# Fourteen weight pieces of an attention and feed-forward kernel: their decoding spread from attention cycle 40 to cycle 58

## The chip, the core and the metric

The kernel runs on one core of a Trainium2 chip. The core has five engines that run side by side, each through its own instruction list in order: TensorE (PE, matrix products; PEld is its loading of weights), VectorE (DVE), ScalarE (ACT), GpSimd (POOL), and SyncE (SP), which here issues the transfers. The metric is the device time of one execution in microseconds (us), the median of several runs.

## What is computed

The input is 64 heads (8 batches of 8) of 576 positions by 64 channels. Attention keeps, in each row of scores, only those within tau of the row's maximum. The result, seen as 4608 tokens by 512 channels, goes through two layers with a slope per hidden unit for negative values.

```python
scores = matmul(q, k.T) / sqrt(64)
thresh = max(scores, -1) - tau
scores = where(scores >= thresh, scores, -1e9)
attn   = softmax(scores)                # 8 x 8 heads, 576 x 576
x      = (attn @ v) as 4608 x 512
h      = x @ w_in                       # 512 x 2048
g      = maximum(h, 0) + alpha * minimum(h, 0)
out    = g @ w_out                      # 2048 x 512
```

The weights w_in and w_out arrive as 64-bit floats.

## The kernel before

**Pairs, units, cycles.** Heads are taken two at a time: 32 pairs, 9 units each (a unit is 128 query rows by 576 keys; one unit of a pair holds what is left over of both heads). The loop at the end of the program runs over cycles i from -3 to 296, and cycle i does the middle step of unit i % 9 of pair i // 9. In it DVE masks the scores of unit i (`mask`, line 438), PE makes the scores of unit i + 2 (`scores`, line 403) and turns the masked rows of unit i by transposes (`turn`, line 447), ACT and DVE copy the turned rows to SBUF, DVE takes the row maximum (`rowmax`, line 418) and ACT the exponential (`expo`, line 426). The scores lie in two PSUM buffers, so that the scores of unit i + 2 wait for the mask of unit i. Products with the values (`avmul`, line 550) come at fixed cycles. Pairs 0 to 3 ("whole") keep the turned rows in one 32-bit copy. From pair 4 on they are split into a high part that ACT copies (line 499) and a rest that DVE subtracts (line 503), one such subtraction per turned tile.

**Fixed order.** The lists of PE, DVE, ACT and POOL are written by hand: what stands earlier in the program text stands earlier in the list. Steps can be set for a cycle by `at_cycle(c, step)`. Transfers on SP are ordered by the compiler.

**Weights.** A weight piece is 128 columns of w_in or 128 rows of w_out, 128x512 words of 64 bits. The class `Split64` turns one into two 32-bit tiles, a high part and a rest. `decode_at(c, ...)` spreads one piece over seven cycles: at c ACT makes two tiles of it (`size`, lines 125 and 126), at c+1 to c+4 DVE has one instruction a cycle (`clamp` line 129, `shift` line 132, `sign` line 137, `power` line 142), at c+4 ACT also rounds (`round`, line 146), at c+5 POOL multiplies and subtracts (`rest`, lines 150 and 151), at c+6 POOL adds (`join`, line 154). These four DVE instructions are called decoding instructions below; i0 to i6 are the pieces of w_in, o0 to o6 those of w_out. A piece of w_in is loaded up to 12 cycles ahead (`LD`), one of w_out 3 cycles ahead. Seven pieces of each weight are decoded during the attention; the other nine of each follow after it and aren't touched by the change.

**Where the words lie.** The raw words of o0 to o5 lie in the place of a later weight tile; those of o6 in a ring of two buffers ("raw") that the loads of q, k and v use as well. The temporary words (`wt`) of a piece lie in a ring of four in the pool `spool`. At cycle 41 (`SPC`) that pool is closed, and its memory goes to the pool `mp1` of the feed-forward part. A piece that begins later takes its temporary words from the ring `g` of `mp1`, which has 11 buffers (`GB`) and otherwise holds the activations between the two layers.

**Feed-forward beside the attention.** As soon as all heads of a batch are done, groups of 256 tokens are fed in: `Mlp.step_l1` (first layer, 7 blocks of 128 hidden units) and `Mlp.step_l2` (second layer), as far as a planner finds room on PE in a cycle (`room`, a budget of 2.6 us). Group 0 is fetched at cycle 49 and its first block starts at cycle 52. A first layer is admitted only while fewer than `GB` activations are in use (`live`). All that is left of the feed-forward follows after the last unit.

The first fourteen pieces before: a piece of w_in every 3 cycles from -3 on, a piece of w_out every 3 cycles from 16 on.

```python
for n_, (w, fc, io) in enumerate(pieces):
    c = DEC0 + DEC * n_ if n_ < F1 else DECO0 + DECO * (n_ - F1)
    load = max(-3, c - LD) if io == "i" else c - 3
    decode_at(c, wp1, w, fc, io, load if n_ else None)
```

Of the kernel before, what the change touches and what calls it, by code (L numbers as in the profile page):

```python
# [25 lines left out]
F1 = 7  # L26
# [9 lines left out]
GB = 11  # L36
# [14 lines left out]
ACTO, SPLO, PUTO = 1, 2, 1  # L51
TH1, TH2, TH3 = 0.75, -0.45, 0.1
XO = 1
L2O = 3
P1 = 2
LD = 12
# [1 line left out]
WHOLE = 4  # L58
EVP = (0, 0, 0, 1)
EVD = lambda i: EVP[i % len(EVP)]  # L60
DEC0, DEC = -3, 3
DECO0, DECO = 16, 3
RDY = 13
CYCLE = 2.6

# [1 line left out]
def f(ap):  # L67
    return ap.bitcast(F32)
# [3 lines left out]
def tile_masked_attention_moe(  # L72
# [31 lines left out]
    class Split64:  # L104
# [12 lines left out]
        def size(self):  # L117
            words = self.raw.bitcast(I32).rearrange("p (n two) -> p n two", two=2)
            self.low, self.high = words[:, :, 0], words[:, :, 1]
            tag, bufs = self.temp_tag  # L120
            pool = self.temp_pool
            if pool is mem:
                pool, tag, bufs = (mem.mp1, "g", GB) if mem.mp1 else (spool, "wt", 4)
            self.t = pool.tile([P, DM], I32, tag=tag, name=f"wt{self.name}", bufs=bufs)
            nc.scalar.activation(f(self.t), f(self.high), AF.Abs)
            nc.scalar.activation(f(self.low), self.low.bitcast(U32), AF.Copy, scale=2.0**-52)

        def clamp(self):
            self.eng[0].tensor_scalar(f(self.t), f(self.t), WORD_LO, WORD_HI, op0=ALU.max, op1=ALU.min)
# [22 lines left out]

        def join(self, lo):
            nc.gpsimd.tensor_tensor(lo, f(self.t), f(self.low), op=ALU.add)

    def src_i(fc):
        return w_in[:, fc * P : (fc + 1) * P].rearrange("(cc p) f -> p cc f", p=P), NCC, f"i{fc}"
# [80 lines left out]
    wp1 = p1.enter_context(tc.tile_pool(name="wp1", bufs=1, side="right"))  # L238
    sp = ExitStack()
    spool = sp.enter_context(tc.tile_pool(name="spool", bufs=1, side="right"))  # L240
    mem = SimpleNamespace(mp1=None)
    at, ps = ExitStack(), ExitStack()
    ap1 = at.enter_context(tc.tile_pool(name="ap1", bufs=1))
    ps_m = ps.enter_context(tc.tile_pool(name="ps_m", bufs=4, space=PSUM))
# [410 lines left out]
    class Mlp:  # L655


        def __init__(self):
            self.l1, self.l2 = deque(), deque()
            self.acc = None  # L660
            self.live = 0
            self.gap = 0
            self.room = 0.0

# [7 lines left out]
        def step_l1(self, i):  # L672
            gi, st, fi = self.l1.popleft()
# [4 lines left out]
                self.gap = i + XO + 2  # L678
                return
            name = f"a{gi}_{fi}"  # L680
            self.live += 1
            ph = layer1(ps_m, fcs1[fi], n, st["x"], name)

            alone = i >= total
# [20 lines left out]
        def step_l2(self, i):  # L705
            _, gi, st, o, fj, ti = self.l2.popleft()
            t0, n = groups1[gi]
            m = min(P, n - o)
            if fj == 0 and ti == 0:
                self.acc = ps_m.tile([P, 512], F32, tag="pm", name=f"acca{gi}_{o}")  # L710
            acc = self.acc
            layer2(acc, fcs1[fj], st["g"][fj], o, m, fj == 0, fj == F1 - 1, (ti,))
            if ti < 2:
                return
            if o + P >= n:
                self.live -= 1
            if fj == F1 - 1:

                def put():
                    po = mem.mp1.tile([P, DM], F32, tag="po", name=f"po{gi}_{o}", bufs=1)  # L720
                    nc.scalar.activation(po[:m], acc[:m], AF.Copy)
                    nc.sync.dma_start(part[gi][o : o + m, :], po[:m])

                first_at_cycle(i + PUTO, put)

        def cycle(self, i, used, slot):

            self.room = min(self.room, TH3) + CYCLE - used
            l1 = False
            if self.l1 and i >= self.gap and self.live < GB:  # L730
                if self.l1[0][2] is None:
                    self.step_l1(i)
                elif slot and self.room > TH1 and ("i", fcs1[self.l1[0][2]]) in ready:
                    l1 = True
                    self.room -= 1.31
# [37 lines left out]
        at_cycle(c + 6, lambda: (w.join((wi if io == "i" else wo)[fc][:, 1]), ready.add((io, fc))))  # L773

    for n_, (w, fc, io) in enumerate(pieces):
        c = DEC0 + DEC * n_ if n_ < F1 else DECO0 + DECO * (n_ - F1)
        load = max(-3, c - LD) if io == "i" else c - 3
        decode_at(c, wp1, w, fc, io, load if n_ else None)

# [259 lines left out]
```

## Time and profile before

| | |
|---|---|
| median of three runs | 1379.86 us (1378.5 to 1380.6) |
| the profiled execution | 1380.41 us, its span 1378.6 us |
| busy in the span | PE 97%, DVE 72%, ACT 61%, POOL 59% |
| chain of work that ended last | PE 85%, DVE 6%, ACT 4% |

The chain of work that ended last is followed back from the last instruction to whatever released each step. Most of the span is PE's. The page's row of DVE shows 6 tenths in the first of 40 slices, 8 or 9 in the next 23, and less behind them; that of PE shows 5 to 8 tenths in the first five slices, and 9 from there on. So the stretch in which PE isn't full is the first 170 us or so, in which the weights are decoded. The time and the span differ by 1.8 us, which lies around the program.

### The profile page before, as it was taken

What the parts mean: (1) busy time and instruction counts of PE and PEld (TensorE: products, weight loads), DVE (VectorE), ACT (ScalarE), POOL (GpSimd) and SP (SyncE); (2) the same over time, 40 slices, a digit from 0 to 9 for tenths busy, and PEclk for the clock granted to TensorE, in tenths of its full rate; (3) what the DMA queues carried; (4) which work ended last, traced back from release to release, by engine and by line L of the source; (5) the groups of instructions that cost most, each with busy time, mean ns of one, the idle gap of its engine ahead of it and who ended that gap; (6) DMA issues with size and microseconds to landing.
All of it is one profiled execution on the core that took longest, in us unless ns stands there. A gap on an engine that the chain in (4) does not pass through costs nothing.

```text
span 1378.6 us, 23959 instructions
## 1 busy us (share of the span) xinstructions
PE 1332.7 (97%) x8116; PEld 1180.2 (86%) x8116; DVE 994.5 (72%) x1970; ACT 842.5 (61%) x1915; POOL 814.9 (59%) x891
## 2 busy tenths in 40 slices
PE   5888899999999999999999999999999999999998
PEld 4556789999999999999999998898888888888887
DVE  6999888888888888889888883883655644333332
ACT  6878888888888888888888873542323321211210
POOL 3776566666666575766666654884757554443431
PEclk9999999999999999999999999999999999999999
DMA  8644643644643644445445413345455452343222
GB/s 252 173 138 112 164 110 109 175 124 112 172 135 114 167 126 128 141 133 142 132 129 150 120 55 110 117 144 169 156 181 187 134 184 92 102 152 113 92 77 77
DMA packets 115178, 186.05 MB, mean 135 GB/s; under 512 B 18320, under 2 KB 49328, under 8 KB 115056
## 3 DMA queue, kind: packets, MB, share of 16 engines
q1 hardware_dynamic: 115056, 184.52, 45.2%
q8 instruction: 65, 1.06, 0.3%
q14 instruction: 57, 0.47, 0.1%
HBM read 104.41 MB, written 37.90 MB: 103 GB/s over the span
## 4 chain that ended last, share of the span: by engine, by line
PE 85%; DVE 6%; ACT 4%; issue 1%; DMA 1%; POOL 1%; SPq 0%; POOLq 0%; DVEq 0%; ACTq 0%
PE accj L232 19%; PE phj L196 18%; PE av L550 11%; PE s L403 11%; PE acca L232 9%; PE pha L196 9%; PE t L447 7%; DVE p L438 2%; DVE nmx L418 1%; PE tk L463 1%; DMA wri<-in_moe_w_in_dram 1%; ACT xb L563 1%; ACT xa L561 1%; ACT xh L182 1%; ACT p L426 0%
## 5 line engine op out<-in xcount | busy, mean ns | idle before, releaser
L418 DVE TENSOR_REDUCE nmx<-s 128x1 f32<-128x576 f32 x288 | 217.2, 754 | 73.2 <-PE s L403 70.1
L223 ACT ACTIVATE gj<-ptj 128x512 fp32r<-128x512 f32 (+1 forms) x109 | 62.9, 577 | 338.1 <-DVE ptj L215 338.1
L226 POOL TENSOR_TENSOR gj<-ptj,gj 128x512 fp32r<-128x512 f32 (+1 forms) x109 | 129.2, 1186 | 237.2 <-ACT gj L223 236.5
L232 PE MATMUL accj<-wo,gj 128*128 128x512 f32 x1140 | 262.4, 390 | 0.6 <-POOL gj L226 0.6
L232 PEld LDWEIGHTS accj<-wo,gj 128*128 128x128 f32 x1140 | 213.9, 188 | 45.1 <-POOL gj L226 1.0
L196 PE MATMUL phj<-xhj,wi 128*128 128x512 f32 (+1 forms) x816 | 232.8, 367 | 0.0
L438 DVE SCALAR_TENSOR_TENSOR p<-s,thr,p 128x576 f32<-128x576 f32 x256 | 206.8, 808 | 1.6 <-ACT thr L431 1.2
L426 ACT ACTIVATE p<-s,nmx 128x576 f32<-128x576 f32 x256 | 190.1, 742 | 10.2 <-DVE nmx L418 9.9
L232 PE MATMUL acca<-wo,ga 128*128 128x512 f32 x588 | 186.1, 423 | 1.6 <-POOL ga L226 0.8
L403 PE MATMUL s<-kh,qst 128*128 128x288 f32 x640 | 142.5, 313 | 38.3 <-DVE p L438 22.1
L196 PEld LDWEIGHTS phj<-xhj,wi 128*128 128x128 f32 x816 | 147.6, 188 | 25.2
L214 DVE TENSOR_SCALAR ptj<-phj,alpha_sb 128x512 f32<-128x512 f32 (+1 forms) x109 | 74.2, 681 | 124.4 <-PE phj L196 120.4
L196 PE MATMUL pha<-xh,wi 128*128 128x256 f32 x784 | 156.9, 284 | 0.2 <-ACT pra L209 0.2
L447 PE MATMUL t<-ident,p 128*128 128x128 f32 x1024 | 154.8, 274 | 0.0
L403 PEld LDWEIGHTS s<-kh,qst 128*128 128x128 f32 x640 | 101.6, 193 | 61.2 <-issue 31.2
L196 PE MATMUL phj<-xlj,wi 128*128 128x512 f32 (+1 forms) x408 | 150.0, 368 | 1.1 <-POOL xlj L810 0.9
L962 DVE TENSOR_TENSOR obj<-accj,pinj 128x512 f32<-128x512 f32 x72 | 49.8, 692 | 138.5 <-PE accj L232 127.7
L403 PE MATMUL s<-kl,qst 128*128 128x288 f32 x640 | 133.7, 299 | 0.0
L196 PEld LDWEIGHTS pha<-xh,wi 128*128 128x128 f32 x784 | 128.1, 190 | 4.4 <-ACT pra L209 1.5
L447 PEld LDWEIGHTS t<-ident,p 128*128 128x128 f32 x1024 | 126.6, 141 | 0.1
L232 PEld LDWEIGHTS acca<-wo,ga 128*128 128x128 f32 x588 | 102.1, 192 | 13.7 <-POOL ga L226 1.2
L219 POOL TENSOR_TENSOR pta<-pta,pra 128x256 f32<-128x256 f32 x94 | 69.4, 739 | 73.9 <-ACT pra L209 71.3
(123 smaller groups left out, 2865.5 us busy)
## 6 DMA issues: line engine op xcount, KB each, us to landing
pinj<-part SPq DMA_DIRECT2D x72, 256.0 KB
kr<-in_k_dram SPq DMA_DIRECT2D x31, 320.0 KB
rb<-rvd SPq DMA_DIRECT2D x64, 144.0 KB
xs<-xa SPq DMA_DIRECT2D x32, 288.0 KB
part<-obj SPq DMA_DIRECT2D x36, 256.0 KB
out_dram<-obj SPq DMA_DIRECT2D x36, 256.0 KB
vr<-in_v_dram SPq DMA_DIRECT2D x28, 320.0 KB
qr<-in_q_dram SPq DMA_DIRECT2D x31, 288.0 KB
```

What stands on the lines that cost most here:

```text
L196: nc.tensor.matmul(ph[:, :n], w[:, c, :], xx[:, c, :n], start=(c == 0 and ti == 0), stop=(c == NCC - 1 and ti == 2),)
L214: nc.vector.tensor_scalar(t[:, :n], ph[:, :n], 0.0, alpha_sb[:, fc : fc + 1], op0=ALU.min, op1=ALU.mult)
L219: nc.gpsimd.tensor_tensor(t[:, :n], t[:, :n], r[:, :n], op=ALU.add)
L223: nc.scalar.activation(g[:, 0, :n], t[:, :n], AF.Copy)
L226: nc.gpsimd.tensor_tensor(g[:, 1, :n], t[:, :n], f(g[:, 0, :n]), op=ALU.subtract)
L232: nc.tensor.matmul(acc[:m, :], gg[:, g, o : o + m], w, start=(first and ti == 0), stop=(last and ti == 2))
L403: nc.tensor.matmul(ps[:, h, :288], w, kk[:, a + h * 288 : a + (h + 1) * 288], start=(ki == 0 and i == 0), stop=(ki == 1 and i == n - 1),)
L418: nc.vector.tensor_reduce(self.nmx[:, j : j + 1], self.S[u][0][:, :, :288], axis=AX.XY, op=ALU.max, negate=True)
L426: nc.scalar.activation(pj, ps[:, :, :288], AF.Exp, bias=nmx[:, j : j + 1], scale=1.0)
L438: nc.vector.scalar_tensor_tensor(pj, ps[:, :, :288], thr[:, j : j + 1], pj, op0=ALU.is_ge, op1=ALU.mult, accum_out=self.sm[:, c : c + 1])
L447: nc.tensor.transpose(tb[:, c, :], pt[:, j, j * D + c * P : j * D + (c + 1) * P], ident)
L550: nc.tensor.matmul(pa[:m, :n], w, x, start=(part == 0 and c == 0), stop=(part == z.parts[-1] and c == NKC))
```

## The change

The four constants that gave each piece its cycle are replaced by a table, with one entry for each of the fourteen pieces. The pieces of w_in now begin every 4 cycles from 1 on (the first stays at -3), o0 to o2 begin at 25, 29 and 34, and o3 to o6 at 41, 44, 48 and 52. The last four therefore take their temporary words from the ring `g`. So that activations and words together don't exceed 11 buffers, the counter `live` is replaced by a list with an entry for each tile taken from the ring, in order. An entry turns true when its tile isn't needed any more, and a first layer is admitted only if all but the last 10 entries are true.

```diff
+ROOM = GB - 1
-DEC0, DEC = -3, 3
-DECO0, DECO = 16, 3
+DECC = (-3, 1, 5, 9, 13, 17, 21, 25, 29, 34, 41, 44, 48, 52)
...
             if pool is mem:
                 pool, tag, bufs = (mem.mp1, "g", GB) if mem.mp1 else (spool, "wt", 4)
+                self.place = None
+                if mem.mp1:
+                    self.place = [False]
+                    mem.ring.append(self.place)
...
             nc.gpsimd.tensor_tensor(lo, f(self.t), f(self.low), op=ALU.add)
+            if self.place:
+                self.place[0] = True
...
-            self.live += 1
+            st["place", fi] = [False]
+            mem.ring.append(st["place", fi])
...
             if o + P >= n:
-                self.live -= 1
+                st["place", fj][0] = True
...
-            if self.l1 and i >= self.gap and self.live < GB:
+            if self.l1 and i >= self.gap and all(p[0] for p in mem.ring[:-ROOM]):
...
-        c = DEC0 + DEC * n_ if n_ < F1 else DECO0 + DECO * (n_ - F1)
+        c = DECC[n_]
```

PE's list is the same, row for row. DVE, ACT and POOL keep their instructions, at other places. The decoding instructions of DVE in the nine cycles of each pair, counted from the two tables (each piece has one at c+1, c+2, c+3 and c+4):

| pair (cycles) | 0 (0-8) | 1 (9-17) | 2 (18-26) | 3 (27-35) | 4 (36-44) | 5 (45-53) | 6 (54-62) |
|---|---|---|---|---|---|---|---|
| before | 12 | 13 | 14 | 12 | 3 | 0 | 0 |
| after | 9 | 9 | 9 | 8 | 6 | 10 | 3 |

DVE's list before at cycles 16 to 20, the end of pair 1 and the start of pair 2 (`wti` and `wto` are temporary words of w_in and w_out, `wri` and `wro` raw words, `p` the exponentials, `nmx` the row maxima, `rv` a pair's sums):

```order
L142 TENSOR_SCALAR wri_264<-wti_622 128x512
L129 TENSOR_SCALAR wti_707<-wti_707 128x512
L438 SCALAR_TENSOR_TENSOR p_3_693,sm_437<-s_8_685,thr_7_691,p_3_693 128x576
L418 TENSOR_REDUCE nmx_0_755<-s_0_716 128x1
L132 TENSOR_SCALAR wti_707<-wti_707 128x512
L129 TENSOR_SCALAR wto_743<-wto_743 128x512
...
L137 SCALAR_TENSOR_TENSOR wti_707<-wri_350,wti_707 128x512
L132 TENSOR_SCALAR wto_743<-wto_743 128x512
L438 SCALAR_TENSOR_TENSOR p_0_758,sm_715<-s_1_750,thr_0_756,p_0_758 128x576
L418 TENSOR_REDUCE nmx_2_820<-s_2_788 128x1
L142 TENSOR_SCALAR wri_350<-wti_707 128x512
L137 SCALAR_TENSOR_TENSOR wto_743<-wro_651,wto_743 128x512
```

The same engine after, at cycles 18 to 20 (the lines of the changed file are 6 to 8 higher: 135, 138, 143 and 148 are the four decoding instructions, 446 the mask, 426 the row maximum):

```order
L135 TENSOR_SCALAR wti_755<-wti_755 128x512
L446 SCALAR_TENSOR_TENSOR p_0_732,sm_697<-s_1_724,thr_0_730,p_0_732 128x576
L426 TENSOR_REDUCE nmx_2_796<-s_2_764 128x1
L138 TENSOR_SCALAR wti_755<-wti_755 128x512
L426 TENSOR_REDUCE nmx_2_796<-s_3_791 128x1
L446 SCALAR_TENSOR_TENSOR p_1_799,sm_697<-s_2_764,thr_2_797,p_1_799 128x576
L515 COPY eo_136<-t_1_802 128x4x128
L143 SCALAR_TENSOR_TENSOR wti_755<-wri_399,wti_755 128x512
```

Before, i6 and o0 overlapped, with two decoding instructions to a cycle; after, one stands in each cycle.

DVE's list before in cycles 45 to 48, at the start of pair 5:

```order
L418 TENSOR_REDUCE nmx_2_1670<-s_2_1647 128x1
L438 SCALAR_TENSOR_TENSOR p_0_1619,sm_1591<-s_1_1623,thr_0_1617,p_0_1619 128x576
L503 TENSOR_TENSOR e_117<-t_0_1655,e_116 128x4x128
L438 SCALAR_TENSOR_TENSOR p_1_1673,sm_1591<-s_2_1647,thr_2_1671,p_1_1673 128x576
L418 TENSOR_REDUCE nmx_2_1670<-s_3_1677 128x1
L503 TENSOR_TENSOR tt_121<-tk_0_1688,tt_120 128x128
L503 TENSOR_TENSOR eo_115<-t_1_1683,eo_114 128x4x128
L418 TENSOR_REDUCE nmx_4_1745<-s_4_1708 128x1
```

And after:

```order
L426 TENSOR_REDUCE nmx_2_1633<-s_2_1604 128x1
L446 SCALAR_TENSOR_TENSOR p_0_1572,sm_1543<-s_1_1576,thr_0_1570,p_0_1572 128x576
L511 TENSOR_TENSOR e_117<-t_0_1612,e_116 128x4x128
L138 TENSOR_SCALAR wto_1598<-wto_1598 128x512
L446 SCALAR_TENSOR_TENSOR p_1_1636,sm_1543<-s_2_1604,thr_2_1634,p_1_1636 128x576
L426 TENSOR_REDUCE nmx_2_1633<-s_3_1640 128x1
L143 SCALAR_TENSOR_TENSOR wto_1598<-wro_1497,wto_1598 128x512
L511 TENSOR_TENSOR tt_121<-tk_0_1651,tt_120 128x128
L511 TENSOR_TENSOR eo_115<-t_1_1646,eo_114 128x4x128
L426 TENSOR_REDUCE nmx_4_1713<-s_4_1674 128x1
```

Two decoding instructions of o4 now stand between the masks, maxima and subtractions. On ACT, in cycle 52, before the high copies (line 507, before 499) of the turned rows, the change puts the rounding of o5 and the two size instructions of o6:

```order
L344 ACTIVATE kh_1890<-kr_1820 128x640
L152 ACTIVATE wo_1895<-wto_1751 128x512
L129 ACTIVATE wto_1897<-wro_1782 128x512
L130 ACTIVATE wro_1782<-wro_1782 128x512
L507 ACTIVATE eo_114<-t_7_1880 128x4x128
```

Before, the key's copy (line 336, after 344) was followed by that high copy at once.

## Rows read from the trace of the kernel before

**Rows 1.** Busy time of each engine in seven stretches, from the first mask of a pair to the first mask of the next: pairs 0 to 6. Columns: stretch, its length, then busy us and instructions of each engine, granted PE clock, DMA share, GB/s.

```profile
14.70:37.00 22.30, 17.56 (x91) 14.06 (x92) 21.33 (x41) 19.27 (x44) 12.56 (x10) 0.92 0.81 249
37.00:63.70 26.70, 24.55 (x134) 15.99 (x133) 24.83 (x48) 22.96 (x53) 18.56 (x16) 1.00 0.61 173
63.70:91.70 28.00, 24.30 (x123) 15.66 (x122) 27.11 (x46) 20.68 (x48) 19.62 (x18) 0.94 0.48 137
91.70:118.00 26.30, 22.42 (x123) 14.83 (x122) 25.12 (x48) 22.53 (x51) 19.88 (x17) 1.00 0.45 128
118.00:141.80 23.80, 20.09 (x124) 15.19 (x122) 21.76 (x49) 19.33 (x45) 13.97 (x13) 1.00 0.41 114
141.80:166.60 24.80, 19.91 (x143) 18.91 (x142) 21.89 (x48) 21.20 (x51) 12.83 (x14) 0.93 0.64 168
166.60:191.00 24.40, 23.32 (x183) 22.60 (x183) 22.61 (x52) 21.19 (x54) 18.05 (x25) 1.00 0.44 120
```

**Rows 2.** DVE's decoding instructions in the stretch of pairs 1 to 3 (37 to 118 us), grouped by line and tile: count, busy us in all, mean ns of one, idle before.

```profile
L129 DVE TENSOR_SCALAR wto<-wto 128x512 f32<-128x512 f32 x7 | 7.2, 1035 | 0.0
L132 DVE TENSOR_SCALAR wto<-wto 128x512 int32<-128x512 int32 x6 | 7.1, 1176 | 0.0
L137 DVE SCALAR_TENSOR_TENSOR wti<-wri,wti 128x512 int32<-128x512 int32 x4 | 5.3, 1334 | 0.0
L137 DVE SCALAR_TENSOR_TENSOR wto<-wro,wto 128x512 int32<-128x512 int32 x6 | 4.2, 697 | 0.0
L142 DVE TENSOR_SCALAR wro<-wto 128x512 int32<-128x512 int32 x6 | 4.1, 692 | 0.0
...
L132 DVE TENSOR_SCALAR wti<-wti 128x512 int32<-128x512 int32 x4 | 2.3, 564 | 0.0
L142 DVE TENSOR_SCALAR wri<-wti 128x512 int32<-128x512 int32 x4 | 2.0, 495 | 0.0
...
L129 DVE TENSOR_SCALAR wti<-wti 128x512 f32<-128x512 f32 x3 | 1.3, 420 | 0.0
```

**Rows 3.** What a piece of w_out costs ACT and POOL in the same stretch, grouped in the same way.

```profile
L126 ACT ACTIVATE wro<-wro 128x512 f32<-128x512 uint32 x7 | 4.7, 672 | 0.0
L125 ACT ACTIVATE wto<-wro 128x512 f32<-128x512 f32 x7 | 4.7, 669 | 0.0
L146 ACT ACTIVATE wo<-wto 128x512 fp32r<-128x512 f32 x6 | 3.7, 622 | 1.3 <-POOL wo L154 1.3
```

```profile
L154 POOL TENSOR_TENSOR wo<-wto,wro 128x512 fp32r<-128x512 f32 x5 | 7.4, 1482 | 0.2
...
L151 POOL TENSOR_TENSOR wto<-wto,wo 128x512 f32<-128x512 f32 x5 | 6.3, 1270 | 1.4 <-ACT wo L146 1.4
...
L150 POOL TENSOR_TENSOR wro<-wro 128x512 f32<-128x512 f32 x5 | 5.7, 1134 | 2.2 <-issue 1.1 <-DVE wro L142 1.0
```

**Rows 4.** Instructions in order of time around 115 us and one at 125.68 us: start, duration, engine, line, tiles.

```profile
114.09 1.56 POOL L340 TENSOR_TENSOR kl<-kr,kh 128x640 fp32r<-128x640 f32 x1 [1.71 <-PE t L447]
...
115.07 0.87 DVE L142 TENSOR_SCALAR wro<-wto 128x512 int32<-128x512 int32 x1
...
115.60 1.49 POOL L154 TENSOR_TENSOR wo<-wto,wro 128x512 fp32r<-128x512 f32 x1
...
115.86 1.52 DVE L129 TENSOR_SCALAR wto<-wto 128x512 f32<-128x512 f32 x1
...
125.68 0.41 DVE L142 TENSOR_SCALAR wro<-wto 128x512 int32<-128x512 int32 x1
```

**Rows 5.** The chain of waits in the stretch of pairs 0 to 3 (14.7 to 118 us): shares of the stretch by engine, tile and line.

```profile
by line: PE s L403 15.4%; PE av L550 13.9%; DVE p L438 13.2%; DVE nmx L418 10.5%; PE t L447 7.1%; DVE wti L137 4.9%; issue 4.3%; DVE wto L129 4.1%; DVE wto L132 3.9%; ACT p L426 2.2%; DVE rv L568 2.2%; DVE wro L142 2.1%; DVE wti L132 1.9%; 
```

**Rows 6.** The same chain in order of time in pair 1, where it runs through PE without a break: start, length, what, instructions.

```profile
44.02 1.01 PE av L550 x4
...
45.23 1.06 PE s L403 x8
...
46.73 1.77 PE av L550 x6
48.50 0.73 PE s L403 x4
49.22 0.43 PE t L447 x4
...
49.77 1.23 PE av L550 x4
...
54.60 1.44 PE av L550 x6
```

**Rows 7.** DVE's waits in the stretch of pairs 4 to 6 (118 to 191 us): who waited for whom, us in all, times, longest.

```profile
DVE nmx L418 <- PE s L403: 3.9, 6, 1.2
DVE eo L503 <- ACT eo L499: 1.6, 5, 0.5
```

**Rows 8.** The query of pair 5, loaded through the ring that o6's raw words share: its issue on SP, and the ACT instruction that reads it, in order of time.

```profile
115.68 0.33 SPq L313 DMA_DIRECT2D qr<-in_q_dram  x1
...
119.48 0.69 ACT L353 ACTIVATE qst<-qr 128x576 fp32r<-128x576 f32 x1
```

**Rows 9.** POOL's subtraction for the first group of the feed-forward, and the first matrix product that reads it.

```profile
158.92 2.40 POOL L184 TENSOR_TENSOR xl<-xr,xh 128x1024 fp32r<-128x1024 f32 x1 [1.21 <-ACT xh L182]
```

```profile
162.80 0.28 PE L196 MATMUL pha<-xl,wi 128*128 128x256 f32 x1
```

**Rows 10.** Busy time as in rows 1, in two stretches of 3.4 us and the ones right behind them.

```profile
66.70:70.10 3.40, 1.13 (x7) 0.70 (x6) 3.40 (x6) 0.37 (x1) 1.69 (x1) 1.00 0.83 251
70.10:73.60 3.50, 3.50 (x13) 2.02 (x12) 3.50 (x8) 3.49 (x8) 3.03 (x3) 0.51 0.73 194
141.80:145.20 3.40, 1.38 (x10) 0.99 (x8) 3.37 (x9) 2.59 (x6) 1.29 (x2) 1.00 0.88 197
145.20:148.70 3.50, 2.83 (x13) 2.85 (x14) 2.83 (x7) 2.08 (x6) 1.41 (x1) 0.51 0.89 273
```

More of the change, by code (lines that the diff above doesn't have):

```diff
@@ L126, in size @@
             nc.scalar.activation(f(self.low), self.low.bitcast(U32), AF.Copy, scale=2.0**-52)
+        place = None
         def clamp(self):
@@ L240, in tile_masked_attention_moe @@
     spool = sp.enter_context(tc.tile_pool(name="spool", bufs=1, side="right"))
-    mem = SimpleNamespace(mp1=None)
+    mem = SimpleNamespace(mp1=None, ring=[])
     at, ps = ExitStack(), ExitStack()
@@ L660, in __init__ @@
             self.acc = None
-            self.live = 0
             self.gap = 0
```

## The prediction

> **What bounds the kernel now.** The chain of waits of the whole run is PE's, but the change touches only the first 60 or so cycles, so I read that part in stretches of one pair each [rows 1]. The reader is to see that DVE, not PE, is full there. In pairs 0 to 3 it is busy in 21.33 of 22.3 us, 24.83 of 26.7, 27.11 of 28.0 and 25.12 of 26.3. PE comes to a like share only in pair 6, with 23.32 of 24.4 us (before, its busy time counts products that wait in its pipeline). PE's list is unchanged, so whatever is won or lost up to cycle 60 shifts all that follows by as much.
>
> What DVE spends on decoding stands in [rows 2]: eight groups, 33.5 us for 40 instructions, so 0.84 us each. That is about twice what one takes when POOL is idle, 0.41 us [rows 4]. The other views that I read are the chain within pairs 0 to 3 [rows 5], that chain in order of time [rows 6], and the waits of DVE in pairs 4 to 6 [rows 7].
>
> **Pairs 0 to 3: work removed.** They lose 3, 4, 5 and 4 decoding instructions, 16 in all (the table in the section on the change). At 0.84 us that is 13.4 us of DVE time. Does it come off the path? For the full price speak pairs 2 and 3, which differ by two decoding instructions and by 28.0 - 26.3 = 1.7 us, 0.85 us each [rows 1]. Both are whole pairs with the same steps in the same cycles. For less speaks the chain [rows 5], which holds the decoding lines at 4.9 + 4.1 + 3.9 + 2.1 + 1.9 = 16.9% of 103.3 us, or 17.5 us. That is 17.5 us for 51 instructions, and 16 of them would be worth 5.5 us. The two ends are 13.4 and 5.5 us.
>
> There is a floor under it. Where the chain runs through PE alone, a cycle takes 0.73 us for scores and 0.43 for transposes, 0.33 more for the leftover unit of a pair (1.06 against 0.73), and a pair has two products of 1.77 + 1.23 us and two of 1.44 + 1.01 [rows 6]. That makes 9 x 1.16 + 0.33 + 6.0 + 4.9 = 21.7 us, and with the small transposes about 22 us for a whole pair. At the full price pairs 1 to 3 would fall to 23.3, 23.8 and 22.9 us. DVE would then need about 21.5 to 23 us of these, so two engines are nearly full and hand over to each other twice a cycle. I take 0.7 us off each of the three for that: **-13.4 + 2.1 = -11.3 us**, nearer to the full price, because the difference of two like pairs is a closer row than a share of a chain.
>
> **Pairs 4 to 6: work added.** The same 16 instructions come back as 3, 10 and 3. DVE has more of its own to do in these pairs (21.76, 21.89 and 22.61 us without or nearly without decoding), since the turned rows are split there. Its idle time is 2.04, 2.91 and 1.79 us, 6.7 in all. Pairs 1 to 3 keep 1.87, 0.89 and 1.18 us idle under full load, 1.3 on the mean, so I count only what is above that as cover: 0.7 + 1.6 + 0.5 = 2.8 us. The price of an instruction depends on POOL, so it is not lower here: pairs 1 to 3 have POOL busy in 58.1 of 81.0 us, 72%. Pair 5 has 12.83 us, gets two and a half pieces of 1.48 + 1.27 + 1.13 = 3.9 us [rows 3], and would have some 22.6 us in 32 or so, 71%. So **+13.4 - 2.8 = +10.6 us**. The lower end is 13.4 - 6.7 = 6.7 us, all idle time used. The upper end is 13.4 plus what ACT adds (second rival).
>
> ACT gets four pieces of 0.67 + 0.67 + 0.62 = 1.96 us, 7.8 us [rows 3], and has 4.5 + 3.6 + 3.2 = 11.3 us idle in pairs 4 to 6 [rows 1]. I cost that at nothing as long as the high copies are not late. If they are, DVE's subtractions wait.
>
> **Steps with one answer.** The list that replaces the counter admits the same layers in the same cycles, for PE's list is the same; four words and seven activations are just 11 buffers, so no tile waits for one: nothing. The raw words of o6 take one of two buffers from cycle 49 to 58, so the query of pair 7 can be loaded only when the key of pair 7 has been read. The same happened before with pair 5: its query was issued at 115.68 us, right behind POOL's reading of the key (114.09 + 1.56), and ACT read it at 119.48 without idling for it [rows 4, 8]. I take nothing, and up to 1 us if SP is held by a transfer of keys in front of it. POOL's subtraction for the first layer ended at 161.32 and PE read it at 162.80 [rows 9]; o4's rest and join come ahead of it, 3.9 us, but the cycles in front of it grow by about as much. Nothing, and up to 1.5 us.
>
> **Sum.** -11.3 + 10.6 = -0.7 us. The profiled execution took 1380.41 us, so 1379.7 in its terms. It lies 0.55 us above the median, which gives **1379.2 us** against 1379.86.
>
> **A rule beside it.** In [rows 4] a decoding instruction that began at 115.86 us ended at 117.38, 0.29 us after POOL's addition (115.60 + 1.49 = 117.09), and the one before it ended 0.29 us after POOL's earlier one (115.94 against 115.65). The Trainium skill (SBUF — State Buffer, section Who interferes with whom) says of this that DVE's two-port instructions and POOL's instructions take one shared pair of ports as an exclusive lock, so that the later one fully blocks. By that rule a decoding instruction is dear or cheap by what POOL has in hand at its start, and one to a cycle instead of two could meet POOL less often. That is the first rival.
>
> **Rivals.** *Faster: fewer meetings with POOL.* An instruction that meets none takes 0.41 us [rows 4], the dearest groups take 1.0 to 1.3 [rows 2]. With two decoding instructions in a cycle the second often starts behind the first under the same POOL work (0.87 and 1.52 us in a row [rows 4]). If one to a cycle brings the mean of all 54 from 0.84 to 0.75 us, that is 4.9 us more: 1379.2 - 4.9 = **1374.3 us**. The double rows in DVE's list before speak for it. Against it speaks that POOL's share doesn't fall. It decides if the mean of the four lines is 0.78 or less.
>
> *Slower: ACT's copies come late in the split pairs.* Rounding and sizing are put in front of high copies on ACT (1.96 us in one go in cycle 52), and DVE's subtraction waits for the copy, with its masks and maxima queued behind it and PE's scores behind those. DVE waits 1.6 us for such copies now [rows 7]. If half of ACT's 7.8 us shows up there, it is 3.9 us: 1379.2 + 3.9 = **1383.1 us**, and 1385.9 us if DVE's idle time takes nothing in as well. ACT's idle time of 11.3 us speaks against it, that DVE already waits there five times speaks for it. It decides from about 3.5 us more of such waits in pairs 4 to 6.
>
> *The clock.* Two stretches in which PE had 1.13 and 1.38 us of work in 3.4 us are each followed by one at half the clock, 0.51 granted, so at 1.2 GHz instead of 2.4 [rows 10]. The first lies where i6 and o0 overlap, and may go. Pair 5, thinner on PE after, may get one more. PE's 2.8 to 3.5 us of work there cost some 1.5 us more than at full clock, so either way the sum moves by about that. It is in the range and no case of its own.
>
> *The change doesn't do what it says.* A wait for one of the 11 buffers would show as ACT waiting before line 129 of a piece. I give it 2 in 100, within the slower case.
>
> **Chances.** The measurement of this kernel can tell about 0.2%, 2.8 us, from no change. My forecast, 1379.2, is within that; its own range is 1376.5 to 1382.5. I give it 43 in 100, the faster case 31, the slower 26. The range for all of it goes from -13.4 + 6.7 = -6.7 us, 1373.2, to the slower case without cover, 1385.9, cut to **1373.5 to 1385.5**: beyond it lie both gains at once, or the small saving of 5.5 us with the full added price, together under 2 in 10.
>
> **What would show it.** Cut by the first masks of the pairs, pairs 0 to 3 should take 92 us instead of 103.3, with DVE over 92% busy in pairs 1 to 3, pair 5 should take 31 to 32 us instead of 24.8 and pairs 4 and 6 about 26 each, and cycle 63 should begin within 3 us of 191.0. The mean of the four decoding lines should stay at 0.8 to 0.9 us; if it falls, the faster case has come. If DVE's waits for ACT's copies grow by several us, it is the slower one. If pairs 1 to 3 stay above 25 us with DVE under 90%, then the floor is PE's or a chain of latencies that I have not seen, and the time is above 1383. If pair 5 takes under 29 us, my price for added work is wrong, and it is below 1376.

## The result, and the profile after

The changed kernel takes **1392.39 us** (median of four runs, 1391.35 to 1395.13) against 1379.94 us (1378.5 to 1380.6) for the kernel before: a ratio of 1.0094, with a 95% interval from 1.008 to 1.0108. It is 12.5 us slower. The forecast was 1379.2 us, and its range ended at 1385.5.

The profiled executions have spans of 1389.6 and 1378.6 us, 11.0 us apart. The stretches that answer to [rows 1], busy time of each engine from the first mask of a pair to that of the next, pairs 0 to 6 (length, PE, PEld, DVE, ACT, POOL, granted PE clock, DMA share, GB/s):

```profile
14.60:38.70 24.10, 19.88 (x99) 15.70 (x100) 21.28 (x39) 18.18 (x43) 11.06 (x9) 1.00 0.69 208
38.70:65.70 27.00, 22.87 (x123) 14.88 (x122) 21.12 (x44) 20.12 (x48) 14.97 (x14) 1.00 0.56 162
65.70:90.40 24.70, 23.34 (x125) 15.16 (x124) 20.04 (x41) 20.44 (x49) 13.05 (x12) 1.00 0.54 159
90.40:116.30 25.90, 22.07 (x121) 14.57 (x120) 23.22 (x42) 20.24 (x47) 14.64 (x14) 1.00 0.49 132
116.30:142.40 26.10, 21.11 (x126) 15.45 (x124) 24.27 (x52) 21.29 (x50) 14.27 (x14) 1.00 0.40 109
142.40:174.50 32.10, 22.82 (x145) 21.22 (x146) 30.34 (x60) 25.58 (x59) 22.92 (x20) 0.89 0.53 150
174.50:202.20 27.70, 22.90 (x178) 21.86 (x177) 25.29 (x56) 21.85 (x53) 23.21 (x30) 1.00 0.36 103
```

Pairs 4 to 6, for which +10.6 us was forecast, grew from 73.1 to 85.8 us, by 12.8. Pair 7 fell from 27.1 to 25.9, since a slow stretch of PE's clock that the kernel before had there is gone (last section). Together, pairs 4 to 7 grew from 100.1 to 111.8 us. Pairs 0 to 3 fell from 103.3 to 101.8 us and not to 92: 1.5 us instead of 11.3. DVE did lose its work in pairs 1 to 3 (64.4 us busy instead of 77.1), but PE didn't get it: DVE has 13.2 us idle there instead of 3.9. From pair 8 on both kernels take 25.3 us a pair, so the 10 us stay to the end.

Where DVE's idle time comes from, the chain of waits shows. Here it is in pair 1 of the changed kernel, in order of time (start, length, what):

```profile
42.33 0.69 ACT qr L366
43.02 0.52 ACT wi L152
43.53 0.56 ACT wti L129
44.10 0.57 ACT wri L130
44.67 0.47 ACT e L515
45.14 0.64 ACT p L434
45.78 0.19 ACT thr L439
45.97 0.03 issue
45.99 0.82 DVE p L446 x2
```

ACT rounds one piece (line 152) and sizes the next (129, 130) in one go, and the exponential that the next mask needs (434) stands behind it. These three instructions in a row are called the bunch below. The pieces begin every four cycles, and rounding comes four cycles after sizing, so the two always meet, and since the pieces begin in odd cycles they meet in those that hold both exponentials of ACT. The same three rows stand in the chain at 19.1, 30.3, 53.9 and 65.2 us. Before, pieces began every three cycles and the two never met for one weight. The waits of ACT and DVE for each other in pair 1 of the changed kernel (who waited for whom: us, times, longest; before, both were 0.8 us):

```profile
ACT p L434 <- DVE nmx L426: 4.9, 6, 1.1
...
DVE p L446 <- ACT thr L439: 2.7, 2, 1.5
```

### The profile page after: what moved, and what is told of

Its sections match the earlier page's. It is cut to its first block, busy times and chain, and to the rows that moved or that the text cites. A ratio compares the mean times of both kernels' runs of the same rounds, so it can differ in the third digit from the quotient of the medians.

```text
span 1389.6 us, 23951 instructions
## 1 busy us (share of the span) xinstructions
PE 1334.5 (96%) x8116; PEld 1180.3 (85%) x8116; DVE 993.8 (72%) x1970; ACT 843.1 (61%) x1915; POOL 814.3 (59%) x891
## 4 chain that ended last, share of the span: by engine, by line
PE 82%; DVE 7%; ACT 6%; issue 2%; POOL 1%; DMA 0%; SPq 0%; POOLq 0%; DVEq 0%; ACTq 0%
PE accj L240 18%; PE phj L204 18%; PE av L558 10%; PE acca L240 10%; PE pha L204 9%; PE s L411 9%; PE t L455 7%; DVE p L446 2%; DVE nmx L426 2%; PE tk L471 1%; ACT p L434 1%; DVE wto L143 1%; ACT xa L569 1%; ACT xb L571 1%; ACT xh L190 1%
## 5 line engine op out<-in xcount | busy, mean ns | idle before, releaser
L426 DVE TENSOR_REDUCE nmx<-s 128x1 f32<-128x576 f32 x288 | 217.1, 754 | 70.7 <-PE s L411 67.6
```

The source lines that it names most:

```text
L426: nc.vector.tensor_reduce(self.nmx[:, j : j + 1], self.S[u][0][:, :, :288], axis=AX.XY, op=ALU.max, negate=True)
```

## The experiments

All are versions of the changed kernel. "Early" pieces are i1 to i6 and o0 to o2, "late" ones o3 to o6. The versions e5 to e13 leave part of the decoding out and serve for timing alone. Lengths are those from first mask to first mask in each trace:

| version | pairs 0-3 | pairs 4-7 | pairs 4-6 alone | time (before beside it) | ratio, interval |
|---|---|---|---|---|---|
| before | 103.3 | 100.1 | 73.1 | | |
| after | 101.8 | 111.8 | 85.8 | 1392.39 (1379.94) | 1.0094, 1.008 to 1.0108 |
| e1, even cycles | 96.2 | 110.5 | 85.1 | 1384.26 (1380.01) | 1.0033, 1.0021 to 1.0044 |
| e2, sizing two cycles ahead | 97.6 | 110.9 | 85.6 | 1385.95 (1380.01) | 1.005, 1.0034 to 1.0067 |
| e3, spacing 3, four late | 99.5 | 109.8 | 83.8 | 1387.49 (1380.01) | 1.0056, 1.0041 to 1.0071 |
| e4, sizing one cycle ahead | 97.5 | 112.5 | 86.5 | 1388.79 (1380.01) | 1.0069, 1.0052 to 1.0086 |
| e5, early without DVE | 96.3 | 109.7 | 84.3 | 1383.93 (1381.19) | |
| e6, early without sizing | 96.5 | 111.9 | 85.9 | 1387.0 (1381.19) | |
| e7, late without DVE | 103.0 | 107.4 | 81.5 | 1388.68 (1381.19) | |
| e8, late without sizing | 103.1 | 110.9 | 85.5 | 1392.15 (1381.19) | |
| e9, late without POOL's rest | 103.4 | 110.2 | 84.5 | 1391.29 (1380.31) | |
| e10, late without DVE and rest | 101.8 | 105.3 | 78.2 | 1385.32 (1380.31) | |
| e11, late bare | 104.7 | 100.8 | 75.1 | 1383.58 (1378.9) | |
| e13, late bare, no transfer | 102.6 | 101.9 | 74.8 | 1382.39 (1378.9) | |
| e12, early bare | 105.1 | 110.6 | 84.7 | 1392.62 (1378.9) | |
| f1, none late, spacing 2 to 3 | 104.0 | 102.0 | 76.3 | 1381.58 (1380.31) | 1.0015, 1.0005 to 1.0025 |
| f4, none late, even cycles | 107.3 | 103.5 | 77.8 | 1387.5 (1380.31) | 1.0052, 1.0036 to 1.0069 |
| f2, o6 alone late, at 44 | 98.3 | 103.5 | 76.4 | 1379.21 (1378.9) | 0.9999, 0.9987 to 1.001 |
| f5, o6 alone late, at 41 | 98.1 | 101.7 | 76.0 | 1378.3 (1379.49) | 0.9988, 0.9979 to 0.9997 |
| f6, o6 alone late, at 64 | 98.1 | 105.0 | 74.3 | 1381.43 (1379.49) | 1.0017, 1.0008 to 1.0026 |

Lengths that nothing in a version touches scatter too: pairs 0 to 3 of e7 to e10 are those of the changed kernel, and give 101.8 to 103.4 us; those of e11 and e13 102.6 to 104.7. So the 1.5 us that the changed kernel wins there lie within this scatter, and the 4 to 6 us that e1, e2 and e4 win over it lie outside. Pairs 4 to 7 with all late work in place (e1 to e6, e12 and the changed kernel) give 109.7 to 112.5 us. Pair 7 has a slow stretch of PE's clock in the kernel before, e10, e13, f2 and f6. Versions with an interval were timed in several runs, the others once.

### Where ACT's steps stand (e1 to e4)

```diff
-DECC = (-3, 1, 5, 9, 13, 17, 21, 25, 29, 34, 41, 44, 48, 52)
+DECC = (-3, 0, 4, 8, 12, 16, 20, 24, 28, 34, 41, 44, 48, 52)   # e1
+DECC = (-3, 0, 3, 6, 9, 12, 15, 16, 19, 22, 41, 44, 48, 52)   # e3
```
```diff
-        at_cycle(c, w.size)
+        at_cycle(c - ahead, w.size)   # third to tenth piece: 2 in e2, 1 in e4
```

e1: 

> The changed kernel with pieces 2 to 9 one cycle earlier, so that their rounding and sizing on ACT fall into even cycles instead of odd ones. Theory A (parity: up to cycle 52 an odd cycle has both exponentials of ACT with the decoding steps between them, an even cycle has none, so 1.96 us of ACT in an odd cycle lie on the chain): pairs 0 to 3 together fall from 101.7 us to 92 to 95, time 1383 to 1386. Theory B (bunch: a spacing of four puts the rounding of one piece and the sizing of the next into one cycle, 1.96 us in one go, whichever cycle it is): no change, 1391 to 1394. Theory C (a floor of latencies in pairs 0 to 3, whatever ACT and DVE have to decode): no change.

e2: 

> The changed kernel with the sizing of pieces 2 to 9 two cycles earlier, DVE's and POOL's steps where they were: sizing and rounding are apart now, but both still in odd cycles. Theory A: no change, 1391 to 1394. Theory B: pairs 0 to 3 fall to 93 to 96 us, time 1384 to 1387. Theory C: no change.

e3: 

> The first ten pieces at the cycles of the kernel before, the last four at 41, 44, 48 and 52 as in the changed one. Pair 3 then has no decoding instruction at all and pair 2 has ten. Theories A and B: pairs 0 and 1 as before (22.3 and 26.7 us), pair 2 some 26, pair 3 some 23 (PE's own 22); pairs 4 to 7 as in the changed kernel, 11 us above before; time 1385 to 1388. Theory C: pair 3 stays at 25 to 26 us without any decoding, time 1390 or more.

e4: 

> The changed kernel with the sizing of pieces 2 to 9 one cycle earlier, in even cycles, and the rounding left in odd ones; DVE's and POOL's steps where they were. Theory A: two thirds of ACT's decoding (1.34 of 1.96 us) leave the odd cycles, time 1385 to 1388. Theory B: 1384 to 1387, as with the sizing two cycles earlier. Theory C: no change, 1391 to 1394.

e1 keeps the bunch and moves it to even cycles, with DVE's and POOL's steps of these pieces one cycle earlier as well; e2 splits it and stays in odd cycles; e4 puts the sizing alone into even cycles. In e2 and e4 DVE's and POOL's steps stay. All three win 4.2 to 5.6 us in pairs 0 to 3. So neither parity alone nor the bunch alone is the cause: it is the bunch between the two exponentials of an odd cycle, and either way out helps. So the "no change" of theory A for e2, of B for e1 and of C for all three is refuted. e4's time, 1388.79 us, lies above the ranges of A and B, as its pairs 4 to 7 took 112.5 us.

e3 asks what one decoding instruction costs, and its expectation miscounts: by the table pair 2 has 13 of them, not ten, and pair 3 none. Pair 3 takes 24.8 us all the same, where A and B expected some 23 and C 25 to 26. Its pairs 2 and 3:

```profile
63.60:89.30 25.70, 21.52 (x118) 14.33 (x118) 25.52 (x45) 19.33 (x45) 18.19 (x17) 1.00 0.48 139
89.40:114.10 24.70, 23.17 (x126) 15.07 (x124) 16.70 (x35) 17.40 (x42) 13.05 (x12) 1.00 0.48 126
```

In e1 ACT has the same instructions in pair 1 as the changed kernel, without those three in front of this exponential (start, length, engine, line, tiles, idle before):

```profile
40.30 0.69 ACT L366 ACTIVATE qr<-qr 128x576 f32<-128x576 f32 x1
40.89 0.57 ACT L515 COPY e<-t 128x512 f32<-128x512 f32 x1
41.36 0.74 ACT L434 ACTIVATE p<-s,nmx 128x576 f32<-128x576 f32 x1
```

And the chain of e1 in pair 1 runs through PE, 44.0 + 29.7 + 14.1 = 88% of it (shares by line):

```profile
by line: PE av L558 44.0%; PE s L411 29.7%; PE t L455 14.1%; issue 3.6%; DVE p L446 3.3%; DVE nmx L426 3.2%; PE tk L471 1.8%; PE rp L581 0.8%
```

### What limits pairs 0 to 3 (e5, e6, e12)

```diff
+        if not bare:                 # e5: not for the second to tenth piece
             at_cycle(c + 1, w.clamp)
             at_cycle(c + 2, w.shift)
             at_cycle(c + 3, w.sign)
             at_cycle(c + 4, w.power)
```
```diff
+            if self.bare:            # e6, in size(): the same pieces
+                return
             nc.scalar.activation(f(self.t), f(self.high), AF.Abs)
             nc.scalar.activation(f(self.low), self.low.bitcast(U32), AF.Copy, scale=2.0**-52)
```
```diff
+                w.t = wi[0][:, 0]    # e12: in place of size() for the same pieces;
+                w.low = wi[0][:, 0]  # no DVE steps and no rest() either
```

e5: 

> The changed kernel without DVE's four decoding instructions of the second to tenth piece (i1 to i6, o0 to o2); that part of the weights' decoding is left out, and ACT's and POOL's steps of these pieces stay where they are. It asks what sets pairs 0 to 3 after the change (101.8 us). If DVE's time still does, pairs 0 to 3 fall by some 8 to 10 us, to the floor of 24 to 25 us for a whole pair that the run with four late pieces showed, 92 to 94 us with the short pair 0. If ACT's steps hold them (rounding of one piece and sizing of the next, 1.96 us in one go between two exponentials), they stay above 98 us although DVE has 29 us less to do. Pairs 4 to 7 stay at 110 to 113 us by both.

e6: 

> The changed kernel without ACT's two sizing instructions of the same nine pieces (that part of the weights' decoding is left out: DVE clamps other words instead, and POOL multiplies the high words by themselves). DVE and POOL keep as many instructions, in the same places. If the jam on ACT takes back the saving, pairs 0 to 3 fall from 101.8 to 97 us or less, as with the sizing moved to other cycles (96.2 to 97.6). If DVE alone sets them, they stay within 1.5 us of 101.8. Pairs 4 to 7 stay at 110 to 113 us by both.

e12: 

> The changed kernel with i1 to i6 and o0 to o2 reduced to the transfer of their raw words, ACT's rounding and POOL's addition; sizing, DVE's four instructions and POOL's multiplication and subtraction are left out, and other words are rounded and added. If 96 us is the floor of the attention itself in pairs 0 to 3, they stay at 95 to 97 us although three engines have 65 us less to do. If POOL's part of the decoding made that floor, they fall to 90 to 93 us.

Taking away DVE's part or ACT's sizing gives the same, 96.3 and 96.5 us, which is also what e1 reaches with all work in place. e5 lies between its two ranges: it keeps the bunch and is as short, so the bunch takes time back only together with the decoding on DVE that stands behind it in the same chain. In e12 pair 0 can't be read: the transfers took more of the DMA engines there (share 1.00 against 0.69 in the changed kernel), and PE waited 11.6 us for a query. Its pairs 1 to 3 can (busy time as above):

```profile
46.40:73.20 26.80, 25.59 (x138) 16.56 (x137) 16.06 (x35) 18.23 (x45) 7.75 (x8) 0.99 0.27 69
73.20:94.90 21.70, 21.55 (x117) 14.10 (x116) 14.65 (x32) 16.95 (x42) 6.85 (x8) 1.00 0.44 122
94.90:119.70 24.80, 23.59 (x131) 15.60 (x130) 16.53 (x35) 18.16 (x43) 10.44 (x11) 1.00 0.47 127
```

They take 73.3 us with PE busy in 70.7, though DVE, ACT and POOL have little else than the attention. e5 and e6 take 73.6 and 73.5 us there, e1 73.9 (pairs 1 to 3 of each in one row):

```profile
37.30:110.90 73.60, 69.41 (x376) 45.52 (x375) 48.49 (x99) 60.26 (x142) 42.08 (x40) 1.00 0.58 162
```
```profile
38.20:111.70 73.50, 68.38 (x368) 44.82 (x368) 63.85 (x125) 53.76 (x128) 43.37 (x39) 1.00 0.57 160
```
```profile
36.60:110.50 73.90, 68.94 (x375) 45.36 (x374) 66.23 (x124) 60.26 (x141) 43.62 (x39) 1.00 0.56 153
```

So PE's floor of pairs 1 to 3 is 73.3 us at most. It may be some 2 us lower (an estimate, 73.3 x 375 / 386): in e12's three rows PE has 386 entries (the x numbers) against 375 in e1's, as it caught up on pair 0 there. Pair 0 stays at 22.3 us or more in all versions: 22.70 in e5, with DVE busy in 15.40 only, so taking DVE's decoding away doesn't shorten it by itself. What holds it isn't shown: e5 has the bunch in its chain at 19.22 us and a slow stretch of PE's clock (0.92 granted), and no version that can be read took both engines' part out.

### What the late pieces cost (e7 to e11, e13)

The edits are those of e5 and e6, for the last four pieces. e9 leaves out `w.rest` alone, e10 that and DVE's four, e11 is e12's edit for the late pieces, and e13 is e11 without `w.load`.

e7: 

> The changed kernel without DVE's four decoding instructions of the last four pieces (o3 to o6); that part of the weights' decoding is left out, ACT and POOL keep their steps. It asks what the 11.7 us that pairs 4 to 7 got longer consist of. If it is DVE's time, as the forecast had it, pairs 4 to 7 fall from 111.8 to 100 to 103 us. If it is ACT's four times 1.96 us in front of the high copies (the slower rival), they fall by 5 us or less. Pairs 0 to 3 stay at 101 to 103 us by both.

e8: 

> The changed kernel without ACT's two sizing instructions of the last four pieces (that part of the weights' decoding is left out: DVE clamps other words instead, and POOL multiplies the high words by themselves). If the late pieces cost DVE's time alone, pairs 4 to 7 stay within 1.5 us of 111.8. If ACT's steps in front of the high copies carry the cost, they fall by 4 to 5 us, that is by about the 5.4 us that ACT has less to do there. Pairs 0 to 3 stay at 101 to 103 us by both.

e9: 

> The changed kernel without POOL's multiplication and subtraction of the last four pieces (o3 to o6); that part of the weights' decoding is left out, DVE's and ACT's steps and POOL's addition stay. Leaving out DVE's 16 instructions took only 4.4 us of the 11.7 us by which pairs 4 to 7 grew, and the chain then ran through POOL in pairs 5 and 6. If DVE is the engine that sets them in the changed kernel and POOL only the next behind it, pairs 4 to 7 fall by 0 to 2 us from 111.8. If POOL sets them as well (by its work in front of the keys, and by making DVE's decoding dear), they fall by 4 to 8 us.

e10: 

> The changed kernel without DVE's 16 decoding instructions and without POOL's multiplication and subtraction of the last four pieces; that part of the weights' decoding is left out, ACT's steps and POOL's addition stay. If DVE and POOL are two limits one behind the other, pairs 4 to 7 fall to 101 to 104 us, by 8 to 11 us, more than either alone. If something else holds them (the loads of the raw words, ACT, the clock), they stay above 106 us.

e11: 

> The changed kernel with the last four pieces (o3 to o6) reduced to the transfer of their raw words, ACT's rounding and POOL's addition; sizing, DVE's four instructions and POOL's multiplication and subtraction are left out, and other words are rounded and added. Without DVE and POOL's part, but with ACT's sizing, pairs 4 to 7 took 105.3 us; before the change they took 100.1. If ACT's sizing carries the rest, they fall to 100 to 102 us. If the transfers or the lists' order carry it, they stay at 104 to 106.

e13: 

> The same as the run with four bare late pieces, and the transfers of their raw words are left out too. If the transfers, or SP held by them, cost time in pairs 4 to 6, pairs 4 to 7 are 1.5 us or more below the run with the transfers; if not, within 1 us of it.

DVE's 16 instructions alone give back 4.4 of the 11.7 us, POOL's rest alone 1.6, ACT's sizing alone 0.9: 6.9 in all. The last two lie within the scatter of the versions with all late work in place (109.7 to 112.5 us), so neither is shown to give anything alone. Together (e11, which also takes no buffers of the ring `g` for these pieces) they give back 11.0. In pairs 4 to 6 alone, clear of pair 7's slow stretch, it is 4.3, 1.3 and 0.3 us, and 10.8 together. Each hides behind the others. e10's 105.3 us lie between its two ranges. Without DVE's part the chain runs through POOL, at the end of e7's pair 5 (start, length, what):

```profile
169.04 1.57 POOL kl L348
170.61 1.00 POOL wro L156
171.61 1.24 POOL wto L157
```

Pair 5 goes from 32.1 us to 30.1 without DVE's part (e7), 28.3 without POOL's rest as well (e10) and 26.4 without sizing (e11):

```profile
142.80:172.90 30.10, 22.33 (x141) 21.55 (x142) 21.92 (x48) 25.92 (x61) 22.06 (x22) 0.83 0.61 161
```
```profile
142.10:170.40 28.30, 20.40 (x141) 19.25 (x142) 22.03 (x48) 25.85 (x60) 15.33 (x16) 0.94 0.62 170
```
```profile
143.60:170.00 26.40, 18.45 (x140) 17.16 (x138) 21.97 (x48) 22.59 (x53) 14.89 (x16) 1.00 0.72 190
```

DVE is busy in about 22 us of all three, so what shortens them isn't DVE. PE's clock differs as well (0.83, 0.94 and 1.00 granted). In e7 it is part of the length: its chain has PE's steps in a slow stretch, four score products in 1.30 us at 159.72 against 0.77 at 146.96. Between e10 and e11 it hardly is, as e13, at 0.93, takes 25.8 us in pair 5. The transfers cost nothing that these runs can tell: e13 without them differs from e11 by +1.1 us in pairs 4 to 7, and pair 7, where it has a slow stretch of PE's clock (last section), is 1.4 us longer.

### Tables with one late piece or none (f1, f4, f2, f5, f6)

```diff
+DECC = (-3, 0, 3, 6, 9, 12, 15, 17, 20, 23, 26, 29, 31, 34)   # f1
+DECC = (-3, 0, 2, 6, 8, 12, 14, 18, 20, 24, 26, 30, 32, 34)   # f4
+DECC = (-3, 0, 3, 6, 9, 12, 15, 18, 21, 24, 27, 30, 34, 44)   # f2; f5 ends with 41, f6 with 64
```

f1: 

> The changed kernel with the table (-3, 0, 3, 6, 9, 12, 15, 17, 20, 23, 26, 29, 31, 34): no late piece, and i6 and o0 begin two cycles apart instead of one. If a moved decoding instruction is worth less in pairs 0 to 3 (a floor of 96 us under them) than it costs in pairs 4 to 7, then the order without late pieces is the better one, and this one keeps within 3 us of the kernel before, 1377 to 1381 us.

f4: 

> The changed kernel with the table (-3, 0, 2, 6, 8, 12, 14, 18, 20, 24, 26, 30, 32, 34): no late piece, every piece but the first begins in an even cycle, so that ACT sizes none in the odd cycles, which hold both exponentials. If the place of ACT's steps is worth 4 to 6 us in pairs 0 to 3, as between the changed kernel and its versions with the sizing moved, and the two dense cycles in six that this table has cost no more than before, it takes 1374 to 1379 us. If two decoding instructions to a cycle are what makes pairs 0 to 3 long, it takes 1380 to 1384 us.

f2: 

> The changed kernel with the table (-3, 0, 3, 6, 9, 12, 15, 18, 21, 24, 27, 30, 34, 44): pieces every three cycles, without the overlap of i6 and o0, and only o6 late. If a late piece costs 2.9 us in pairs 4 to 7 and each of the four instructions that leave pairs 0 to 3 saves what it did with even cycles (7.1 us for 16, 0.44 us each, 1.8 us a piece), it takes 1380 to 1382 us. If one late piece is hidden by the idle time of pairs 4 to 6, it takes 1376 to 1379 us.

f5: 

> The table with one late piece, with o6 at cycle 41 instead of 44: DVE's four instructions fall in cycles 42 to 45, the end of pair 4, POOL's in 46 and 47. If the price of a late piece is DVE's, it is the same there, 3 to 4 us in pairs 4 to 7, and the time 1379 to 1380.5 us. If pair 5 is the dear place, pairs 4 to 7 take 100 to 102 us instead of 103.5 and the time is 1376 to 1378 us.

f6: 

> The table with one late piece, with o6 at cycle 64: DVE's four instructions fall in cycles 65 to 68, pair 7, POOL's in 69 and 70; one block of a first layer moves behind some products of the second layer in PE's list. Pairs 5 and 6 fall back to 24.5 to 25 us. If PE, nearly full there, hides the piece, pair 7 stays at 27 us or below and the time is 1375 to 1377.5 us. If a late piece costs 3 us anywhere, pair 7 takes 28 to 30 us and the time is 1378 to 1380 us.

f1, f4 and f6 came out above all their ranges, f2 and f5 between theirs. f1 and f4 lose in pair 3 (30.4 and 31.3 us). Their tables put two decoding instructions into its first cycle, 27, which also has the sums of the pair before (`rv`); in the other tables that cycle has one or none. In f1's chain there (start, length, what) three decoding instructions, the first still of cycle 26, take 4.5 of 6.9 us:

```profile
86.31 1.87 DVE wto L143
88.17 0.74 DVE p L446 x2
88.91 0.67 DVE nmx L426
89.58 0.77 DVE rv L576
90.34 0.02 issue
90.37 0.22 DVE rv L577
90.58 1.17 DVE wro L148
91.75 1.42 DVE wto L135
```

That this cycle is the cause was read from the chain and not tried alone, and f1 itself speaks against it as the whole cause: by its table cycle 18 is as full, and its pair 2 takes 25.0 us. Pair 3 has PE's clock at 0.94 granted in f1 and 0.89 in f4. f4's even cycles for ACT didn't make up for it. One late piece and even spacing of three cycles give 98.1 to 98.3 us in pairs 0 to 3, 5 us less than before. At 44 it gives 3.4 us of that back, at 41 1.6, at 64 4.9 (pair 7 grew to 30.7 us, at 0.89 granted clock, and PE's list differs there a little). Most of the difference between 44 and 41 is pair 7's slow stretch, which f2 has (27.1 us) and f5 hasn't (25.7): in pairs 4 to 6 they give back 3.3 and 2.9 us. Even that isn't shown to be the late piece's, for f1 and f4 have none and take 3.2 and 4.7 us more there than the kernel before. f5 is the only version whose interval lies below 1, by 1.2 us, which is less than the 0.2% named in the forecast; it is about 1% below the changed kernel (0.9988 against 1.0094).

## Why the prediction was wrong

**The step that failed** is the saving in pairs 0 to 3, "-13.4 + 2.1 = -11.3 us". Measured: -1.5, within the scatter. Three errors are in it.

*Pair 0.* It was to lose three instructions at 0.84 us, 2.5 us. It lost nothing in any version, even without nearly all of its decoding on DVE (e5). That DVE was busy in 21.33 of 22.3 us [rows 1] was taken for the one limit. It wasn't; what else holds pair 0 stays open.

*The price.* The full 0.84 us rested on pairs 2 and 3 of the kernel before, 1.7 us apart for two decoding instructions. But pair 2 had a slow stretch of PE's clock (0.94 granted, pair 3 1.00) [rows 1], which wasn't taken off. In e3, at 1.00, pair 2 takes 25.7 us with 13 instructions and pair 3 24.8 with none: 0.9 us for 13. The other end, 5.5 us by the share of the chain, was the nearer one to e1's 7.1.

*ACT in pairs 0 to 3.* The sum costed ACT's steps in pairs 4 to 6 only, and left out where the new table puts them before. The forecast had pairs 1 to 3 at 24.0 + 24.5 + 23.6 = 72.1 us; with ACT's steps out of the way they take 73.9 (e1), 1.8 us more. What stops them there is the floor and not the price, for without DVE's decoding it is 73.6 (e5). The changed kernel takes 77.6: the bunch on ACT takes back 3.7 us there and 1.8 in pair 0. With the 2.5 us of pair 0 and the 1.8 of the floor these are the 9.8 us between -11.3 and -1.5. What the bunch takes back is shown three ways: moved (e1, e4), split (e2) and left out (e6).

**The added work in pairs 4 to 6**, +10.6 us, was near in size (+12.8) and wrong in kind, so the size came out in part by luck. It was worked out as DVE's time. DVE's part alone accounts for 4.3 us there; the rest needs POOL's and ACT's shares gone as well. ACT's 7.8 us were costed at nothing because ACT had 11.3 us idle. Its sizing, 5.4 us of them, is worth 3.1 us in these pairs once DVE and POOL are out of the way (e10 against e11), and nothing clear of the scatter with them in place (e8). ACT's idle share said little about that. Of the steps costed at nothing, one shows a wait: ACT waited 0.8 us for the query of pair 7, within the "up to 1 us" allowed.

**The rivals.** *Fewer meetings with POOL*: the mean of the four decoding lines in pairs 1 to 3 went from 0.84 to 0.80 us (21.5 us for 27), above its mark of 0.78. Pair 5 has prices of 0.40 to 1.79 us (count, busy, mean ns):

```profile
L143 DVE SCALAR_TENSOR_TENSOR wto<-wro,wto 128x512 int32<-128x512 int32 x3 | 5.4, 1788 | 0.0
...
L135 DVE TENSOR_SCALAR wto<-wto 128x512 f32<-128x512 f32 x3 | 2.3, 778 | 0.0
...
L148 DVE TENSOR_SCALAR wro<-wto 128x512 int32<-128x512 int32 x3 | 1.2, 398 | 0.0
```

*Copies late in the split pairs*: DVE's waits for the high copies are 2.0 us in pairs 4 to 6 against 1.6 [rows 7], far from the 3.5 us more that it needed. ACT did decide the sign, but in pairs 0 to 3 and by the exponential. The prediction's own test named the outcome: pairs 1 to 3 above 25 us on the mean with DVE under 90% (25.9 us, 83%) meant that "the floor is PE's or a chain of latencies that I have not seen". It was the chain, through ACT.

*The clock*: the kernel before has four slow stretches up to pair 7, the changed one two, both in pair 5. The forecast left such shifts in its range. The one that is gone from pair 7 made the changed kernel 1.2 us shorter there.

**What stays open.** What a single late piece costs isn't separated from the scatter in pairs 4 to 6 and from the clock's slow stretches, of which f5 has one up to pair 7 (7 us long), f2 three and the kernel before four. Nor is it shown what holds pair 0, and what made pair 3 of f1 and f4 long.

## What to carry to other kernels

When a step is moved to another cycle, cost it on every engine that has a part of it, at every place where it lands, and look which instruction stands right behind it in that engine's list: 1.7 us of spare work in front of one exponential took back most of what the emptier DVE could have given (5.6 of 7.1 us, e1). A table with a fixed spacing makes the steps of neighbouring pieces meet always or never, so look at spacing and length of the recipe together. And where work is added on three engines at once, leaving it out on one shows only the next: the single effects add up to less than the whole. Before a difference of two stretches is read as a price, see whether both ran at the same granted clock.

## What the runs showed of the hardware

**A decoding instruction under POOL.** In pair 5 of the changed kernel, POOL's and DVE's instructions in order of time (start, length, engine, line, tiles):

```profile
150.16 1.30 POOL L160 TENSOR_TENSOR wo<-wto,wro 128x512 fp32r<-128x512 f32 x1
...
156.38 1.41 POOL L602 TENSOR_TENSOR xa<-xa,xb 128x576 f32<-128x576 f32 x1
...
163.11 2.36 POOL L192 TENSOR_TENSOR xl<-xr,xh 128x1024 fp32r<-128x1024 f32 x1
```
```profile
150.28 1.74 DVE L143 SCALAR_TENSOR_TENSOR wto<-wro,wto 128x512 int32<-128x512 int32 x1
...
156.59 1.49 DVE L135 TENSOR_SCALAR wto<-wto 128x512 f32<-128x512 f32 x1
...
163.33 2.70 DVE L143 SCALAR_TENSOR_TENSOR wto<-wro,wto 128x512 int32<-128x512 int32 x1
```

The two signs end 0.56 us after POOL's instruction (152.02 against 151.46, 166.03 against 165.47), the clamp 0.29 us after (158.08 against 157.79), whatever the length of POOL's. These are three cases. So the dearest, 2.70 us, is that which met POOL's longest. This agrees with the exclusive lock that the Trainium skill states (SBUF — State Buffer, section Who interferes with whom).

**A slow stretch of PE's clock cost 1.4 us in a pair that PE fills.** Pair 7 has one in some versions, 3.4 us at 0.51 granted, so at 1.2 GHz instead of 2.4. Of the kernel before, pair 7 and the stretch itself; of e11, which has none there, pair 7:

```profile
191.00:218.10 27.10, 25.02 (x177) 23.80 (x176) 22.64 (x52) 22.02 (x54) 18.74 (x24) 0.94 0.42 114
196.50:199.90 3.40, 3.40 (x18) 3.40 (x17) 1.79 (x5) 2.33 (x6) 3.16 (x3) 0.51 0.65 137
```
```profile
194.20:219.90 25.70, 23.61 (x177) 22.28 (x176) 22.59 (x52) 21.99 (x54) 18.69 (x24) 1.00 0.44 120
```

PE has 1.41 us more to do for the same 177 groups, and the pair is 1.4 us longer. Differences of 1 to 2 us between versions in pairs 4 to 7 can be this. Where PE isn't full, a slow stretch need not cost anything: pair 5 takes 25.8 us with one in e13 (0.93 granted) and 26.4 without in e11.
